# The same instructions in another order: an attention and expert-mixing kernel whose step order becomes a written list

## The chip, the cores and the metric

One core of one Trainium2 chip runs the whole program. The metric is device time in microseconds (us). Before the change three runs took 616.56 to 617.46 us, with a median of 617.3 us. The trace is of one profiled execution.

## The reference

Two stages follow each other. In the first, 64 heads (8 batches of 8, 576 positions of 64 numbers) go through a linear attention: q and k are projected to 128 features, the greatest absolute value of each row is taken off, and both signs of the exponential are kept.

```python
def phi(x):
    proj = np.einsum('bhsd,df->bhsf', x, w_phi)
    proj = proj - np.max(np.abs(proj), axis=-1, keepdims=True)
    return np.concatenate([np.exp(proj), np.exp(-proj)], axis=-1)
kv = np.einsum('bhsf,bhsd->bhfd', k_p, v)      # and z, the sum of k_p over s
num = np.einsum('bhsf,bhfd->bhsd', q_p, kv)    # divided by q_p . z
```

Its result x (8 batches of 576 x 512) goes through four softmax attentions, the experts, with a causal mask; for each position the two experts with the greatest gate logits are kept, weighted by a softmax over the two, and added after the projection `wo`.

```python
q, k, v = x @ wq[e], x @ wk[e], x @ wv[e]
a = softmax(where(causal, -1e9, 0.125 * q @ k.T))
out += gate_weight[e] * (a @ v @ wo[e])
```

## The kernel before, in words

The program is written as some twenty kinds of generators ("streams"). Each yields a `Step` that names the engine of the next piece of work, and then issues that piece. A `Plan` chooses which stream goes on next; the choice fixes the order in which every engine executes its instructions, since `in_order` (called at the end) ties each instruction to the one before it on its engine. No loop remains at run time.

The first stage works in 32 pairs of heads (p). `load_k`, `load_q` and `load_v` issue the transfers, on SyncE's queue but for the first two loads of q. `stream_k` projects k (line 509, a tiling of TensorE with 64 rows), `center` takes the greatest absolute value and subtracts it (VectorE, lines 564 and 578), ScalarE makes both exponentials (326); `key_sum` adds blocks of them on VectorE (546), and `stream_kv` multiplies them with v in four tiles of 32 columns (605, 622). The product is transposed on TensorE for the first six pairs (633), later on VectorE and through DRAM (641, `kvd`). `stream_q` projects q (509); `evac_u` copies the result from PSUM to `u`, on ScalarE (324) or VectorE (336); GpSimd finds the greatest value over all partitions (`partition_all_reduce`, 681); VectorE subtracts it (685); ScalarE makes the exponentials (326). `stream_n` makes the denominators (710) and numerators (721), also in 32-column tiles; `fractions` and `divide` form the quotient and split it into two parts, `xh` and `xl`.

The second stage works in 8 batches of 4 pairs, each batch in two groups of two experts, which makes 16 groups (n = 0 to 15). Products with `qk`, `vg` and `wo` use the full 128 x 128 tiling, three products of high and low parts each (315). The scores use 64-row tiles (838). Then follow the copy from PSUM (324 or 336), the mask on GpSimd (942), maxima on VectorE (955), an all-reduce on GpSimd into the one buffer `max` (959), the subtraction (963), exponentials (326), the addition of blocks into that same buffer `max` (975), their sums on TensorE (1001), the product with v (1030), `evac_y` (1044, 324, 319), the projection with `wo` (315), `evac_o` and the stores, which go through two buffers `ot`. A new all-reduce can overwrite `max` only after the sums of the group before have read it.

What sets the order before: `Plan.loop` estimates for each stream when its step could start, from assumed costs, keeps those within `WINDOW` of the earliest, and takes the one of the lowest position number. These numbers come from tables (`POS`, `POS1`, `BOFF`, `MOVE`) by pair and batch. Where a step may go to either engine (`copies`), the estimate also picks ScalarE or VectorE, with 544 ns against VectorE (`FLEX`). `keep_warm` fills TensorE with small products until the first x exists.

Of the kernel before, what the change touches and what calls it, by code (L numbers as in the profile page):

```python
# [12 lines left out]
ALU = mybir.AluOpType  # L13
# [5 lines left out]
NP = H // 2  # L19
# [21 lines left out]
HOT = 22.62  # L41
SLOPE = (-27.1, -45.11, 31.37, 22.04, 0.2)
# [5 lines left out]
FLEX = (544, -30)  # L48
QB = 1
PSUB = 0  # L50
# [4 lines left out]
WINDOW = 53.0  # L55
SWITCH = 43.0
SLACK = 150.0
LATE = (1200.0, 500.0)
PHASE = 0.0
ZEROS = 34.47  # L60

MOVE = {
# [10 lines left out]
    'evu': (21.12, -4.06, 14.36, -18.44, 5.1, 15.91, 29.23, -7.85, 16.87, -12.86, 9.23, -24.49, -1.82, -0.22, -20.76, 24.81, 11.28, -7.35, 2.92, 2.45, 9.93, -6.72, -3.41, -34.68, -21.04, 1.48, -2.83, 22.44, -22.76, -6.25, 15.97, -11.69,),  # L73
    'ph0': (-8.14, 0.95, 0.11, -1.26, 2.32, -7.14, 14.26, 1.03, -4.68, 5.71, 17.28, -2.71, 7.54, -8.69, 8.12, 18.24, -7.03, 16.87, -6.18, -9.54, -25.96, 24.71, -7.89, 12.56, -1.56, 10.54, -2, -6.36, -29.4, -8.19, -24.29, 4.42,),
    'ph1': (0.98, -31.26, 7.61, 13.17, -13.03, -6.78, -4.19, 30.31, 1.24, 14.84, -16.58, -8.83, -2.18, 2.26, -24.69, 4.64, 4.19, -14.28, -5.42, 5.41, 8.16, -8.76, -6.61, 2.72, -6.37, 21.76, -7.17, -16.16, -0.85, 16.73, 11.84, -11.68,),
    'cen': (-18.81, 6.49, -10.84, 12.73, -20.02, 8.22, 2.67, -4.13, -37.26, -31.66, -22.98, -21.09, -1.99, 11.55, -10.57, 24.02, 3.96, -3.59, 2.44, 14.24, 5.39, 33.73, 12.84, 2.35, -5.61, -5.03, -22.36, 21.58, -8.41, -5.42, -15.78, 16.67,),
    'evd': (-0.53, -8.66, 7.47, -22, -18.99, -9.4, -18.15, 12.47, -19.84, 8.28, -2.9, -3.62, 17.77, 27.72, -5.5, -22.57, 11.69, -3.3, -11.95, -21.43, -1.49, 34.49, 13.92, 18.59, 3.14, 4.37, 4.81, 2.48, 26.02, 6.28, 12.39, -10.59,),
    'n1': (7.63, -9.91, 2.94, 8.61, 6.97, 3.71, 0.17, -10.61, -19.77, -1.78, -4.43, -30.48, -18.43, 0.14, 9.45, -11.23, -16.35, -18.78, 7.28, 10.47, 7.42, -28.12, 5.4, 14, -24.35, -5.88, -12.01, -7.61, 17.16, -5.33, -22.39, -11.91,),
    'div': (-24.16, 1.89, 13.29, 2.53, 0.65, -0.28, 8.21, -7.67, -3.37, 4.47, -12.51, 7.23, 1.58, -6.78, 5.93, 2.54, 10.1, -14.14, -5.17, -6.51, 26.08, -8.09, -24.63, 7.57, 4.12, 2.66, -35.81, -1.48, 11.92, -19.86, -16.37, -36.85,),
# [6 lines left out]
    'gate': (19.49, -11.43, -6.09, 0.85, 5.59, 17.09, 4.34, 6.95,),  # L86
    't1': (6.21, -13.36, 7.09, -2.21, -6.96, -5.15, -13.11, -22.93,),
    'out': (0.94, -2.47, -1.22, -1.17, -4.2, 1.36, 15.49, 6.05,),
    'fin': (0, 0, 0, 0, 0, 0, 0, -0.18,),
}  # L90
POS1 = {'wq': 24.27, 'wv': 48.25, 'wo': 6.32, 'n0': -29.41, 'n1': 1.65, 'k': -1.55, 'q': -17.83, 'v': 6.22, 'kv': -23.07, 'z': 0.35, 'cen': -7.3, 'evu': -37.47, 'ph0': 25.81, 'ph1': 20.93, 'div': 3.92, 'evd': -3.25, 'lk': -12.81, 'lq': 47.36}
BOFF = (-5.07, 0.34, -2.66, -3.42, -4.38, 5.28, 25.26, 8.75)

POS = {'fin': 20.11, 'p0': -6.7, 'p1': -66.09, 'v0': 14.93, 'gate': -16.07, 's0': 3.48, 's1': -24.31, 'm0': 14.77, 'm1': 13.89, 't0': -38.13, 't1': 12.5, 'out': 23.34}
NPAIRS = B * NP
HEAD = 2.29
# [3 lines left out]
TRATE = 2.37  # L100
CHANGE = (150.0, 190.0)
PORT = 350.0
OTHER = 20.47
LDW = 109.0
PSUM_TILES = (("c", 8, 512),)


def moved(x, i):

    return MOVE[x][i] if x in MOVE else 0  # L110


def of_pair(x, p):

    return (p - HEAD if p < NP else p) + POS1[x] + moved(x, p)


def of_batch(x, b):
    return NP * b + BOFF[b] + POS[x] + moved(x, b)


class Step:

    def __init__(self, eng, needs=(), tag=None, pred=None, hot=False, port=False, tiling=(128, 128), n=1, slack=0.0, filler=False):
        self.eng, self.needs, self.tag, self.pred = eng, needs, tag, pred
        self.port, self.tiling, self.n = port, tiling if eng == 'PE' and (tag or tiling != (128, 128)) else None, n
        self.lead = HOT if hot else 0.0
        self.filler = filler  # L130
        self.slack = slack + (SLACK if eng == 'PE' else 0.0)


class Plan:


    HOP = {'PE': 200.0, 'DVE': 150.0, 'ACT': 150.0, 'POOL': 80.0, 'SP': 100.0}

    def __init__(self):
        self.warm, self.busy = False, []  # L140
        self.tiling = None
        self.rings = 0.0
        self.free = {e: 1470.0 if e == 'PE' else 600.0 for e in ('PE', 'DVE', 'ACT', 'POOL', 'SP')}
        self.ready = {}
        self.last = {}
        self.psum = {}
        self.streams = []
        self.pool = []
        self.done = set()
# [17 lines left out]
    def blocked(self, t):  # L167

        return PORT if any(a < t < b for a, b in self.pool) else 0.0

    def run(self, eng, cost, w=(), r=(), rows=128, tiling=(128, 128), port=False):
        if eng == 'PE' and tiling != self.tiling:
            cost += CHANGE[tiling == (128, 128)]
            self.tiling = tiling
# [7 lines left out]
        if port:  # L182
            cost += self.blocked(t)
        end = t + cost
        self.free[eng] = end
        if eng == 'POOL':
            self.pool = [*self.pool[-7:], (t, end)]
# [21 lines left out]
    def after(self, table, k, eng):  # L209
        t, by = table.get(k, (0.0, eng))  # L210
        if by == eng == 'PE':
            return t
        return t + self.HOP[by] + (100.0 if eng == 'PE' else 0.0)

    def spawn(self, gen, pos):
        s = [gen, None, pos]
        if self.advance(s, None):
            self.streams.append(s)

    def advance(self, s, value):  # L220
        try:
            s[1] = s[0].send(value)
            if isinstance(s[1], tuple):
                s[1], pos = s[1]
                s[2] = s[2] if pos is None else pos
# [931 lines left out]
```

## Time and profile before

| | |
|---|---|
| median of three runs | 617.3 us |
| profiled execution, span | 615.0 us |
| around the span, if that execution took the median | 2.3 us |
| TensorE busy | 600.5 us, 98% |
| VectorE busy | 557.3 us, 91% |
| ScalarE busy | 432.0 us, 70% |
| GpSimd busy | 245.0 us, 40% |
| chain that ended last | TensorE 74%, VectorE 15%, ScalarE 5% |

PE is TensorE, DVE VectorE, ACT ScalarE, POOL GpSimd, SP SyncE. Matmuls overlap in their pipeline, so the sum of their durations is more than the time that they take: what one costs in a row of equal ones is the distance between starts. The page does not give the profiled execution's whole time, only its span; the difference to the median is carried along unchanged.

### The profile page before, as it was taken

Reading aid. Unit: us, or ns where it says so; the run is one execution under the profiler, and the core shown is the slowest. Engines: PE = TensorE matmul, PEld = TensorE weight load, DVE = VectorE, ACT = ScalarE, POOL = GpSimd, SP = SyncE. Lnnn points to the kernel's source line nnn. Section 1 sums busy time; section 2 is a strip of 40 time slices with the busy share of each in tenths; the row PEclk is TensorE's granted clock in tenths of the full one; section 3 lists DMA queues with packets and bytes.
Section 4 is the critical chain, followed back from the end, with each engine's and each line's share of the span. In section 5 each row is a group of like instructions: output and inputs, shape, how many; then the busy total and the mean of one; then the engine's idle time right before and its main releaser. Section 6 shows DMA issues by size and latency. Waiting matters only on the chain.

```text
span 615.0 us, 19992 instructions
## 1 busy us (share of the span) xinstructions
PE 600.5 (98%) x8263; PEld 470.6 (77%) x8263; DVE 557.3 (91%) x1124; ACT 432.0 (70%) x1034; POOL 245.0 (40%) x167
## 2 busy tenths in 40 slices
PE   8999999999999999999999999999999999999987
PEld 7665788667796778768886868876889677878976
DVE  5899989999999999999899999999999998888793
ACT  4898786667687688677775885875796668556652
POOL 5635533453324644252333614418430706421420
PEclk9999999999999999999999999999999999999999
DMA  9553212253113431253214332144212311020022
GB/s 218 155 150 103 59 51 81 68 159 87 54 66 113 120 87 37 72 158 110 74 35 107 119 107 63 46 135 138 66 53 83 111 37 27 15 92 2 2 78 78
DMA packets 41610, 52.48 MB, mean 85 GB/s; under 512 B 21168, under 2 KB 24624, under 8 KB 41520
## 3 DMA queue, kind: packets, MB, share of 16 engines
q1 hardware_dynamic: 41200, 50.62, 28.5%
q8 instruction: 65, 1.06, 0.7%
q10 hardware_dynamic: 320, 0.59, 0.4%
q14 instruction: 25, 0.20, 0.1%
HBM read 36.64 MB, written 14.55 MB: 83 GB/s over the span
## 4 chain that ended last, share of the span: by engine, by line
PE 74%; DVE 15%; ACT 5%; DMA 2%; issue 2%; POOLq 1%; POOL 1%; SPq 0%; ACTq 0%; DVEq 0%
PE ps_c L315 29%; PE ps_c L509 9%; PE ps_c L605 9%; PE ps_c L721 7%; PE ps_c L1030 6%; PE ps_c L838 6%; PE ps_c L710 4%; DVE u L685 3%; DVE zs L546 2%; PE ps_c L622 2%; ACT ek L326 2%; PE ps_c L1001 1%; DVE s L963 1%; DVE ek L578 1%; DVE max L975 1%
## 5 line engine op out<-in xcount | busy, mean ns | idle before, releaser
L681 POOL PARTITION_ALL_REDUCE mx<-u x64 | 144.2, 2305 | 182.7 <-ACT u L324 165.9
L315 PE MATMUL ps_c<-xh,qk 128*128 128x320 f32 (+1 forms) x512 | 106.1, 298 | 0.0
L959 POOL PARTITION_ALL_REDUCE max<-top x16 | 59.9, 3745 | 101.5 <-DVE top L955 35.8
L315 PEld LDWEIGHTS ps_c<-xh,qk 128*128 128x128 f32 x512 | 82.7, 188 | 2.3 <-issue 0.7
L326 ACT ACTIVATE ek<-ek 128x1152 f32<-128x1152 f32 x64 | 75.0, 1171 | 5.7 <-DVE ek L578 5.0
L315 PE MATMUL ps_c<-xl,qk 128*128 128x256 f32 (+1 forms) x256 | 75.5, 295 | 0.0
L605 PE MATMUL ps_c<-ek,v_in 128*32 128x256 f32 x1280 | 75.4, 381 | 0.0
L963 DVE TENSOR_TENSOR s<-s,max 128x1152 f32<-128x1152 f32 (+4 forms) x80 | 68.3, 879 | 1.0 <-POOL max L959 1.0
L942 POOL TENSOR_SCALAR_AFFINE_SELECT s<-s 128x256 f32<-128x256 f32 (+1 forms) x80 | 41.5, 558 | 62.2 <-ACT s L324 61.9
L685 DVE TENSOR_TENSOR u<-u,mx 128x576 f32<-128x576 f32 x64 | 61.6, 975 | 3.9 <-POOL mx L681 3.9
L324 ACT COPY s<-ps_c 128x512 f32<-128x512 f32 (+4 forms) x152 | 52.7, 445 | 14.7 <-PE ps_c L838 14.4
L326 ACT ACTIVATE s<-s 128x1152 f32<-128x1152 f32 (+4 forms) x80 | 56.4, 740 | 8.6 <-DVE s L963 8.4
L605 PEld LDWEIGHTS ps_c<-ek,v_in 128*32 128x32 f32 x1280 | 39.7, 110 | 27.2 <-issue 1.3
L315 PE MATMUL ps_c<-vg,xh 128*128 128x260 f32 (+1 forms) x320 | 58.9, 286 | 0.3 <-ACT s L324 0.3
L564 DVE TENSOR_REDUCE pmax<-ps_c 128x4 f32<-128x512 f32 (+1 forms) x96 | 49.5, 539 | 8.1 <-PE ps_c L509 8.0
L315 PE MATMUL ps_c<-yh,wo 128*128 128x320 f32 (+1 forms) x256 | 53.1, 303 | 0.0
L326 ACT ACTIVATE mx<-u 128x576 f32<-128x576 f32 x64 | 43.9, 687 | 10.5 <-DVE u L685 10.4
L324 ACT COPY u<-ps_c 128x256 f32<-128x256 f32 (+1 forms) x127 | 41.6, 412 | 11.7 <-PE ps_c L509 11.4
L578 DVE TENSOR_TENSOR ek<-ps_c,pmax 128x512 f32<-128x512 f32 (+1 forms) x96 | 49.8, 537 | 0.0
L315 PEld LDWEIGHTS ps_c<-vg,xh 128*128 128x128 f32 (+1 forms) x320 | 47.4, 177 | 1.9 <-ACT s L324 0.8
L509 PEld LDWEIGHTS ps_c<-wf,k_in 64*128 64x128 f32 x576 | 41.9, 190 | 8.5 <-ACT u L324 3.0
L509 PE MATMUL ps_c<-wf,k_in 64*128 64x128 f32 x576 | 46.7, 283 | 1.5 <-ACT u L324 1.1
(124 smaller groups left out, 1399.4 us busy)
## 6 DMA issues: line engine op xcount, KB each, us to landing
v_in<-in_v_dram SPq DMA_DIRECT2D x32, 320.0 KB, 3.0
out_dram<-ot SPq DMA_DIRECT2D x32, 288.0 KB, 2.1
q_in<-in_qt_dram SPq DMA_DIRECT2D x60, 144.0 KB, 2.9
kvd<-kvt SPq DMA_DIRECT2D x104, 48.0 KB, 1.7
kv<-kvd SPq DMA_DIRECT2D x26, 192.0 KB, 2.6
k_in<-in_kt_dram SPq DMA_DIRECT2D x32, 144.0 KB, 2.8
k_in<-in_kt_dram SPq DMA_DIRECT2D x32, 128.0 KB, 2.8
q_in<-in_qt_dram ACTq DMA_DIRECT2D x4, 144.0 KB, 4.1
```

The costliest lines, as they stand in the source:

```text
L315: nc.tensor.matmul(o, a, b, start=start, stop=stop, skip_group_check=True)
L324: nc.scalar.copy(o, i)
L326: nc.scalar.activation(o, i, func, **kw)
L509: nc.tensor.matmul(o, a, b, start=True, stop=True, skip_group_check=True)
L564: dve(n * 128, [mk], [pk]).tensor_reduce(out=m[:, us], in_=src, axis=AX.X, op=ALU.max, apply_absolute_value=True)
L578: dve(n * 128, [e1k], [pk, mk]).tensor_tensor(out=ek2[p % EKB][:, 1, us, :], in0=src, in1=m[:, us].unsqueeze(2).to_broadcast([128, n, 128] ...
L605: nc.tensor.matmul(o[g, 0:2], v_in[:, 4 * h + t if t < 4 else 8 + h, k:64:2], ek[:, :, u_, :].rearrange("p c (w f) -> p c w f", w=4), star ...
L681: nc.gpsimd.partition_all_reduce(M, U, 128, bass_isa.ReduceOp.absmax)
L685: (nc.gpsimd if st.eng == 'POOL' else nc.vector).tensor_tensor(out=U, in0=U, in1=M, op=ALU.subtract)
L721: nc.tensor.matmul(ps[g:g + 32, 0:n], kvi[:, 2 * k + h, 32 * c:32 * c + 32], P_[h][c][:, s0:s1], start=c == 0, stop=c == 1, skip_group_che ...
L959: nc.gpsimd.partition_all_reduce(big.rearrange("p e s -> p (e s)"), top.rearrange("p e s -> p (e s)"), 128, bass_isa.ReduceOp.max)
L963: dve(2 * (S - 128 * j), [('d', x, j)], [('max', z)], 1.11, True).tensor_tensor(out=block(s_, j, None, rows(j)), in0=block(s_, j, None, ro ...
```

## The change

The tables and the choice go. Two strings stand in their place. Each character of `ORDER` is an index into the list of live streams, and the stream at that index goes on; each character of `SIDES` says for one step that could go either way whether it goes to ScalarE (0) or VectorE (1). The pieces of work, the tiles, buffers and transfers are those of before; the assumed costs in `plan.run` were changed as well, and still choose which free PSUM bank a step gets. The only instructions that differ in number are the fillers of `keep_warm` (117 before, 105 after), and 64 copies out of PSUM or between buffers that stand on VectorE instead of ScalarE (31 on VectorE before, 95 after).

```diff
+ORDER = (
+    r'11000000320000063655BEEE???66BA2B?@3BA555500EGG?00000000000000@A0B047D073DD0@@@?:@25766A@16:00:7I:ADC?4B6A5B15'
...
+SIDES = (
+    r'10000010101100000100011001000100000001011000000000001001001000000000000110000000000010000000000000000000000000'
...
     def loop(self):
-        while self.streams:
-            cand = []
...
-                t, eng = self.start(st)
-                cand.append((t + (SWITCH if st.filler or self.other(st) else 0.0), eng, s))
...
-            t0 = min(c[0] for c in cand) + WINDOW
-            _, eng, s = min((c for c in cand if c[0] <= t0), key=lambda c: (round(1e4 * (c[2][2] - c[2][1].lead + (OTHER if self.other(c[2][1]) else 0.0))), c[0]))
-            s[1].eng = eng
+        sides = iter(SIDES)
+        for c in ORDER:
+            s = self.streams[ord(c) - 48]
+            st = s[1]
+            assert st.pred is None or st.pred()
+            if isinstance(st.eng, tuple):
+                st.eng = st.eng[int(next(sides))]
             slot = None
...
     def copies(n):
-        return ('ACT', 52 + 0.83 * n), ('DVE', 65 + 1.04 * n + FLEX[0])
+        return 'ACT', 'DVE'
```

Line numbers of the changed kernel are some 36 to 46 lower than those of before: 509 is 471, 838 is 792, 315 is 279, 685 is 645, 963 is 917, 975 is 929, 1001 is 955, 1030 is 984.

First place, TensorE in the first third: the last block of a projection of k (one product with `wf` that stands alone). Before, it comes between the key sums and a numerator:

```order
L509 MATMUL ps_c3_66<-wf_118,k_in0_102 128x128
L622 MATMUL ps_c2_65<-zs_111,ones_112 32x4x32 x4
L622 MATMUL ps_c2_65<-ek0_108,sel_114 32x4x32 x4
L509 MATMUL ps_c4_67<-wf_118,k_in0_102 128x128
L721 MATMUL ps_c6_69<-mx30_139,kv1_120 32x256 x2
```

Now, at a like place of a later pair, such a block stands between two runs of scores:

```order
L792 MATMUL ps_c2_65<-qh0_159,kkl0_162 128x320
L792 MATMUL ps_c0_63<-ql0_160,kkh0_161 128x320
L792 MATMUL ps_c2_65<-ql0_160,kkh0_161 128x320
L471 MATMUL ps_c6_69<-wf_118,k_in1_103 128x128
L792 MATMUL ps_c7_70<-qh0_159,kkh0_161 128x448
```

What moved: the single block left a stretch of 32-column tiles, where it made TensorE change its tiling twice, for a stretch of 64-row tiles like its own. Counted over the whole order (64-row tiles of both lines taken as one kind, 32-column tiles as a second, full tiling as a third), the tiling changes 169 times before and 144 times after; behind the last scores 7 and 5 times.

Second place, VectorE behind the last scores (group 15, in s1; s0 holds group 14). Before:

```order
L955 TENSOR_TENSOR top0_155<-s1_154 128x2x448
L955 TENSOR_TENSOR top0_155<-top0_155,s1_154 128x2x320
L955 TENSOR_TENSOR top0_155<-top0_155,s1_154 128x2x192
L955 TENSOR_TENSOR top0_155<-top0_155,s1_154 64x2x64
L963 TENSOR_TENSOR s0_153<-s0_153,max0_156 64x2x64
L975 TENSOR_TENSOR max0_156<-s0_153 128x2x448
L975 TENSOR_TENSOR max0_156<-max0_156,s0_153 128x2x320
```

Now (909 is 955, 929 is 975):

```order
L909 TENSOR_TENSOR top0_155<-s1_154 128x2x448
L909 TENSOR_TENSOR top0_155<-top0_155,s1_154 128x2x320
L929 TENSOR_TENSOR max0_156<-s0_153 128x2x448
L929 TENSOR_TENSOR max0_156<-max0_156,s0_153 128x2x320
L909 TENSOR_TENSOR top0_155<-top0_155,s1_154 128x2x192
L909 TENSOR_TENSOR top0_155<-top0_155,s1_154 64x2x64
```

The two additions for group 14 moved ahead of the last two maxima of group 15, and the small subtraction of group 14 to an earlier place. On TensorE the sums that read these additions stand right behind the product with `vg` after the change; before, two units with `wo` stood between.

Third place, VectorE behind the last all-reduce, from the third subtraction of group 15 on. Before:

```order
L963 TENSOR_TENSOR s1_154<-s1_154,max0_156 128x2x320
L742 TENSOR_TENSOR ps_c7_70<-ps_c7_70,gc_166 128x18
L963 TENSOR_TENSOR s1_154<-s1_154,max0_156 128x2x192
L745 STREAM_TRANSPOSE rb0_157<-ps_c7_70 128x576
L963 TENSOR_TENSOR s1_154<-s1_154,max0_156 64x2x64
L975 TENSOR_TENSOR max0_156<-s1_154 128x2x448
L1044 TENSOR_TENSOR ps_c2_65<-ps_c2_65,rb0_157 128x256
L1044 TENSOR_TENSOR ps_c4_67<-ps_c4_67,rb0_157 128x320
L975 TENSOR_TENSOR max0_156<-max0_156,s1_154 128x2x320
```

Now:

```order
L917 TENSOR_TENSOR s1_154<-s1_154,max0_156 128x2x320
L917 TENSOR_TENSOR s1_154<-s1_154,max0_156 128x2x192
L917 TENSOR_TENSOR s1_154<-s1_154,max0_156 64x2x64
L702 TENSOR_TENSOR ps_c6_69<-ps_c6_69,gc_166 128x18
L929 TENSOR_TENSOR max0_156<-s1_154 128x2x448
L929 TENSOR_TENSOR max0_156<-max0_156,s1_154 128x2x320
L705 STREAM_TRANSPOSE rb0_157<-ps_c6_69 128x576
L998 TENSOR_TENSOR ps_c0_63<-ps_c0_63,rb0_157 128x256
```

The transpose into `rb0` and the two multiplications of group 14 moved behind both additions of group 15. On TensorE, the product of group 15 with v now follows its sums directly; before, two half units with `wo` (six products) stood between them.

## Rows read from the trace of the kernel before

**Rows 1.** The page, its first line and its busy times:
```profile
span 615.0 us, 19992 instructions
PE 600.5 (98%) x8263; PEld 470.6 (77%) x8263; DVE 557.3 (91%) x1124; ACT 432.0 (70%) x1034; POOL 245.0 (40%) x167
```

**Rows 2.** Windows: length, busy time (and instructions) by engine, granted clock, DMA share, GB/s:
```profile
30.00:585.00 555.00, 549.23 (x7549) 428.96 (x7542) 517.02 (x1029) 400.10 (x963) 223.45 (x152) 1.00 0.28 80
...
598.00:602.50 4.50, 3.20 (x34) 2.54 (x38) 2.64 (x7) 1.54 (x6) 0.00 (x0) 0.62 0.17 66
```

**Rows 3.** Chain that ended last, pieces on TensorE: start, us, what:
```profile
10.10 4.29 PE ps_c L315 x75
...
183.94 1.80 PE ps_c L315 x12
185.74 2.84 PE ps_c L1030 x56
188.58 1.94 PE ps_c L721 x32
...
387.37 7.33 PE ps_c L315 x60
394.70 2.08 PE ps_c L721 x32
396.78 2.16 PE ps_c L605 x40
```

**Rows 4.** Timeline around 221 to 226 us, GpSimd, VectorE, TensorE (start, us, instruction, idle):
```profile
221.25 4.47 POOL L681 PARTITION_ALL_REDUCE mx<-u  x2 [8.45 <-ACT u L324]
...
221.52 1.85 DVE L685 TENSOR_TENSOR u<-u,mx 128x576 f32<-128x576 f32 x1
223.47 0.44 DVE L732 STREAM_TRANSPOSE wided<-ps_c 128x288 f32<-128x288 f32 x1
223.91 1.58 DVE L685 TENSOR_TENSOR u<-u,mx 128x576 f32<-128x576 f32 x1
225.42 0.77 DVE L745 STREAM_TRANSPOSE rb<-ps_c 128x576 f32<-128x576 f32 x1
...
226.24 0.47 PE L838 MATMUL ps_c<-qh,kkh 64*128 64x448 f32 x1 [1.26 <-DVE rb L745]
```

**Rows 5.** Instructions of tile u on VectorE: duration ns min/median/max:
```profile
L685 DVE TENSOR_TENSOR u<-u,mx x64: 709/747/2255, 11.5 to 519.5; 128x576 f32<-128x576 f32 x64
L336 DVE COPY u<-ps_c x1: 474/474/474, 413.7 to 413.7; 128x320 f32<-128x320 f32 x1
```

**Rows 6.** Groups by line and shape: busy us, mean ns, idle before:
```profile
L685 DVE TENSOR_TENSOR u<-u,mx 128x576 f32<-128x576 f32 x64 | 61.6, 975 | 3.9 <-POOL mx L681 3.9
L732 DVE STREAM_TRANSPOSE wided<-ps_c 128x288 f32<-128x288 f32 x32 | 15.0, 467 | 1.1 <-PE ps_c L710 1.0
```

**Rows 7.** Chain that ended last, from the last scores on:
```profile
575.94 2.66 PE ps_c L838 x35
...
581.44 1.16 DVE top L955
...
585.94 0.84 DVE max L975
...
588.31 3.65 POOLq L1152
...
595.63 0.69 DVE rb L745
...
597.94 0.49 DVE ps_c L1044
598.43 0.74 DVE max L975
...
599.30 1.40 PE ps_c L1001 x24
600.70 1.74 PE ps_c L315 x6
602.44 2.84 PE ps_c L1030 x56
```

More of the change, by code (lines that the diff above doesn't have):

```diff
@@ L99, with change_cost @@
 RATE = 2.18
[L100 to L103, printed above, removed]
+TRATE = 2.4
+EXIT = 95.0
+ENTRY = {'F': 102.0, 'R': 99.0, 'S': -31.0, 'C': 23.0, 'Q': 10.0}
 LDW = 109.0
+ROWS = (0.997, 1.008)
 PSUM_TILES = (("c", 8, 512),)
[L108 to L119, printed above, removed]
-class Step:
[L126 to L131, printed above, removed]
+def change_cost(a, b):
+    if a is not None and a[:2] == b[:2]:
+        return 0.0
+    kind = ('C' if b[0] == 128 else 'Q') if b[1] < 128 else 'F' if b[0] == 128 else 'S' if len(b) > 2 else 'R'
+    return EXIT + ENTRY[kind]
@@ L181, in run @@
             cost = self.clocked(t, cost, rows)
-        if port:
+        if eng == 'DVE' and port:
             cost += self.blocked(t)
+            self.shared = (t, t + cost)
+        if eng == 'POOL' and self.shared[0] < t < self.shared[1]:
+            t = self.shared[1]
         end = t + cost
@@ L231, in release @@
         self.psum[tag].append(t)
-    def start(self, st):
-        best = None
-        for eng, cost in st.eng if isinstance(st.eng, tuple) else ((st.eng, 0.0),):
-            t = self.free.get(eng, 0.0)
-            for k in st.needs:
-                t = max(t, self.after(self.ready, k, eng) + st.slack)
-            if st.tag is not None:
-                t = max(t, sorted(self.after(self.last, k, eng) for k, _ in self.psum[st.tag])[st.n - 1])
-            if eng == 'DVE' and st.port:
-                cost += self.blocked(t)
-            if best is None or t + cost < best[0]:
-                best = t + cost, t, eng
-        return best[1:]
@@ L506, in half_mm @@
     def half_mm(o, a, b, n, w, r, alone=1.0):
-        plan.run('PE', 2 * alone * n / TRATE + 3, [w], r, tiling=(64, 128))
+        plan.run('PE', alone * ROWS[n == 128] * (2 * n / 2.37 + 3), [w], r, tiling=(64, 128))
         nc.tensor.matmul(o, a, b, start=True, stop=True, skip_group_check=True)
@@ L531, in stream_k @@
             cols = [slice(0, 9)] if not CACT else [slice(4 * t, min(9, 4 * t + 4)) for t in range(3) if t not in CACT]
-            yield Step('ACT', [e1k], pred=lambda: all(('center', p, t) in done for t in range(3)))
+            yield Step('ACT', pred=lambda: all((('center', p, t) in done for t in range(3))))
             for us in cols:
@@ L608, in stream_kv @@
             if adds:
-                yield Step('PE', ['zs'], pred=has('zs', p), hot=True, slack=LATE[1], tiling=(128, 32))
+                yield Step('PE', pred=has('zs', p))
             first = 1 if KADD == 3 else 2
@@ L895, in gates @@
         G = 'gate'
-        yield Step('DVE', ['lg'], pred=lambda: all(('v', b, j) in done for j in range(NJ)) and (not b or ('gate', b - 1) in done))
+        yield Step('DVE', pred=lambda: all((('v', b, j) in done for j in range(NJ))) and (not b or ('gate', b - 1) in done))
         dve(80, [G], ['lg'], port=True).tensor_tensor(out=ge, in0=lg.unsqueeze(3).to_broadcast(sh4),
@@ L917, in gates @@
         done.add(('gw', b))
-        kc, ps = yield Step('PE', [G], 'c', tiling=(128, 32), slack=LATE[0])
+        kc, ps = yield Step('PE', 'c')
         o = ps[:, 0:40].rearrange("p (g j a d) -> p g j a d", g=2, a=2, d=2)
@@ L924, in gates @@
             nc.tensor.matmul(o[r:r + 32, :, :, a, half], ident[:, c:c + 32], w2[:, e], start=True, stop=True, skip_group_check=True)
-        st = Step(copies(40), [kc], pred=lambda: not b or (('gated', 2 * b - 1) in done and ('gated', 2 * b - 2) in done), hot=True)
+        st = Step(copies(40), pred=lambda: not b or (('gated', 2 * b - 1) in done and ('gated', 2 * b - 2) in done))
         yield st
@@ L938, in mask @@
         sk = [('S', x, IN_BANK[j][0], e) for e in range(2)]
-        yield Step('POOL', sk, pred=lambda: all(('S', n, IN_BANK[j][0], e) in done for e in range(2)))
-        plan.run('POOL', 260 + 1.3 * 2 * w, [('m', x, j)], sk)
+        yield Step('POOL', pred=lambda: all((('S', n, IN_BANK[j][0], e) in done for e in range(2))))
+        plan.run('POOL', 230 + 0.65 * 2 * w, [('m', x, j)], sk, port=100 + 1.3 * w)
         d = ss[x][:w, :, KEYS[j]:KEYS[j] + w]
@@ L989, in sums @@
         s_, need = ss[x], [('P', x, 0)] + ([('max', n % MB)] if SADD else []) + [('P', x, j) for j in range(SADD + 1, NJ)]
-        pk, ps = yield Step('PE', need, 'c', lambda: ('acc', n) in done and all(('P', n, j) in done for j in range(NJ)), tiling=(128, 32)), of_batch(f't{g}', b)
+        pk, ps = yield Step('PE', 'c', lambda: ('acc', n) in done and all((('P', n, j) in done for j in range(NJ))))
         pieces = [(block(s_, j), 64 * j, j == 0, j == NJ - 1) for j in range(NJ)]
```

313 lines of the change are left out of this document (152 added, 161 removed), and 16 rows, old and new, of the table MOVE.

## Prediction
> **What bounds the kernel now.** I read the page's busy times first, then the windows, then the chain of waits, and last the timelines at places where TensorE waits. TensorE is busy for 600.5 of 615.0 us, VectorE for 557.3, ScalarE for 432.0 [rows 1]. The middle part, from 30 to 585 us, is 555.0 us long, and TensorE idles there for 555.0 - 549.2 = 5.8 us, VectorE for 555.0 - 517.0 = 38.0 us [rows 2]. So over nine tenths of the run the end is set by how fast TensorE gets through its list. What an order can win there is of two kinds: the cost of changing the tiling, which hides inside "busy", and the few waits. The reader should see in the chain that a block of equal products costs more when it follows another tiling: 32 numerator products take 2.08 us behind the full-tiling product with `wo` or `qk`, and 1.94 behind other 32-column products; 56 products with v take 2.84 behind the full tiling [rows 3].
>
> Behind the last scores, which end at 575.94 + 2.66 = 578.60 us, the picture changes: 36.4 us of the span are left, and most of that is a chain through VectorE, GpSimd and TensorE for the last group of experts [rows 7]. [...]
>
> A third thing can be seen at 221 to 226 us. A subtraction on VectorE (line 685) that usually takes 747 ns [rows 5] takes 1.85 and 1.58 us while GpSimd's all-reduces run, the transpose into `rb` queues behind it, and TensorE idles 1.26 us for that transpose [rows 4]. VectorE's busy time thus holds time in which it is only held up. For line 685 alone that is 64 x (975 - 747 ns) = 14.6 us [rows 5, 6].
>
> **The change part by part.** All sums start from the profiled execution: 615.0 us of span, and 2.3 us around it if it took the median of 617.3.
>
> *Tiling changes.* I counted them in the two orders: 169 and 144, of which 7 and 5 stand behind the last scores; 23 fewer in the part that TensorE bounds. The price of one: 2.08 - 1.94 = 0.14 us [rows 3]. The single projection block between scores in the new order shows how they were saved. Entering the full tiling may cost a little more and leaving it less; both ends of the price, 0.05 and 0.25 us, are my estimate around that one difference. 23 x 0.14 = 3.2 us less (1.2 to 5.8).
>
> *Fillers.* 12 fewer; 75 took 4.29 us [rows 3], so 12 x 0.057 = 0.7 us. They only fill time in which TensorE waits for the first pairs, so the gain may be nothing. I take 0.7.
>
> *Waits in the middle.* 5.8 us are visible [rows 2]. A wait costs more than its idle time, since the pipeline fills again: the product behind the wait at 226.24 us took 0.47 us [rows 4], where products in a full row start 7.33 / 60 = 0.12 us apart [rows 3]. About 0.35 us for each of some eleven waits gives 3.8 us, together 9.6 us at most. At the other end the new order has as many waits as the old one, and the gain is nothing (it can be below nothing: that is the third rival). No row shows the new waits. I take the middle, 4.8 us, because the visible wait that I followed came from a held-up subtraction, and an order can set such a subtraction beside the all-reduce or behind it.
>
> *Copies that move to VectorE.* 64 copies; the one of this kind in the trace took 474 ns for 320 columns [rows 5], and many are shorter, so 0.43 us each, 27.5 us (64 x 0.474 = 30.3 at most). They leave ScalarE, which had 30% of its time free. On VectorE they fall into 38.0 us of idle time and into the 14.6 us and more in which two-input operations are held up. I cost them at nothing for the end; the cover is that idle time, and if it is gone they cost up to 27.5 us. Queued behind each of them on VectorE are the subtractions, additions and row maxima that give back PSUM banks, and TensorE waits for those.
>
> [...] In rows 4 the transpose into `wided`, which reads PSUM, ran in 0.44 us under an all-reduce, no slower than its mean of 467 ns [rows 6], while the subtraction of two SBUF tiles was held up. [...]
>
> *The tail.* First, the last all-reduce starts 588.31 - 578.60 = 9.7 us after the last scores [rows 7]. Its maxima begin at 581.44, and with the two additions the row of VectorE ends at 585.94 + 0.84 = 586.78, of which some 0.2 us is the small subtraction that now stands earlier; but it still had to wait until TensorE had done two units with `wo` and the sums of group 14. Now 60 products with `vg` follow the scores, 60 x 0.12 = 7.3 us, and then the sums at once, about 1.1 us: all-reduce at 8.5 us behind the scores, 1.2 us earlier. Second, from the chain between all-reduce and the last additions, the transpose into `rb` (0.69 us) and a multiplication (0.49 us) are gone: 1.2 us. Third, six products between the sums and the product with v (1.74 us at the lower clock) are gone: 1.7 us. They come later, where stores already set the pace; I give back 0.5 us. Together 1.2 + 1.2 + 1.7 - 0.5 = 3.6 us less (1.5 to 5.5). Late next are the last two multiplications of group 14, now behind the additions; they have the 2.84 us of the product with v [rows 7] to be done in.
>
> *Sum.* 615.0 - 3.2 - 0.7 - 4.8 - 3.6 = 602.7 us of span; with 2.3 us around it 605.0 us.
>
> **The rivals.** *Only what can be counted.* The waits of the middle stay: 617.3 - 3.2 - 0.7 - 3.6 = 609.8 us. For it: two in-order engines at 98% and 91% leave little room, and one stall moved is often another made. Against it: TensorE's waits have few and plain causes.
>
> *Nearly all waits go.* 617.3 - 3.2 - 0.7 - 9.6 - 3.6 = 600.2 us, and with the upper ends of the tail and the tiling price 598. For it: all waits together are under 2% of the span. Against it: the first 60 us, in which VectorE and ScalarE feed the first pairs, leave no choice.
>
> *VectorE becomes the bound (slower).* The place is the middle part. If VectorE is held up as often as before, 27.5 of its 38.0 us of idle time go, 10.5 us or 2% are left, and an in-order engine with so little slack is late for the row maxima, the subtractions and the quotients. If half of the added work then shows up as waits of TensorE, the time is 617.3 - 7.5 + 13.7 = 623.5 us. It decides as soon as more than 7.5 us of new TensorE waits appear. For it: VectorE is the next busiest engine, and the change loads it. Against it: the held-up time can shrink by about as much as is added.
>
> *The order does nothing.* Waits that the list did not foresee eat the counted gains: 616 to 618 us. Against it: fewer tiling changes are certain, and the tail is a chain of single rows.
>
> **How the numbers follow.** The forecast of 605.0 us gets 0.47, only the countable parts 0.19, nearly all waits 0.14, VectorE as the bound 0.13, nothing 0.07. About 0.2% of the time, 1.2 us, can be told from no change. Faster: 0.47 + 0.19 + 0.14 + 0.01 = 0.81; the same 0.05; slower 0.13 + 0.01 = 0.14. The range for 8 in 10 goes from 598 us, the bottom of the third case, to 616 us, which leaves out VectorE as the bound and most of the last case. The forecast's own range is 602 to 608.
>
> **What would show it.** Right: the last scores end near 570 us instead of 578.6; between them and the end of the span about 33 us; TensorE's idle time in the middle falls to about 3 us; the mean of the subtraction (now line 645) falls from 975 towards 800 ns; no stretch at the lower clock, or a shorter one, before the last product with v. VectorE's busy time then stays below 575 us. Wrong: VectorE's busy time at 585 us or more, with TensorE waits on VectorE that sum to over 10 us, would be the third rival; a last all-reduce that starts 9.7 us or more behind the last scores would refute the tail; equal TensorE waits with a gain near 7 us would be the first rival.

## The result and the profile after

The changed kernel takes 624.62 us (median of four runs, 623.74 to 625.54) against 616.93 us before (614.86 to 617.46): ratio 1.0131, 95% interval 1.0109 to 1.0154. It is 1.3% slower, where 2% faster was forecast. The profiled execution took 624.03 us, 2.4 us of it outside the span (2.3 had been carried along for before). The two spans differ by 6.6 us, the medians by 7.7.

The page of the changed kernel, its first line, busy times, and the chain that ended last by engine and by line:

```profile
span 621.6 us, 20010 instructions
...
PE 600.5 (97%) x8251; PEld 468.9 (75%) x8251; DVE 590.5 (95%) x1188; ACT 404.8 (65%) x970; POOL 248.6 (40%) x167
...
PE 51%; DVE 32%; issue 8%; POOL 5%; ACT 2%; DMA 1%; SPq 1%; DVEq 0%; ACTq 0%; POOLq 0%
PE ps_c L279 17%; PE ps_c L471 7%; PE ps_c L681 6%; PE ps_c L567 6%; DVE zs L508 6%; PE ps_c L792 4%; PE ps_c L984 4%; DVE u L645 4%; PE ps_c L670 3%; DVE s L917 3%; DVE top L909 3%; POOL mx L643 3%; DVE pmax L526 2%; DVE ek L540 2%; PE ps_c L584 1%
```

TensorE is busy as long as before [rows 1]; VectorE 33.2 us longer. VectorE's part of the chain has doubled from 15% to 32%, and its largest line there is 508, the key-sum additions. The windows of the changed kernel (columns as in [rows 2]):

```profile
30.00:585.00 555.00, 541.03 (x7449) 419.56 (x7451) 538.41 (x1072) 367.17 (x885) 224.86 (x148) 1.00 0.29 82
...
600.00:606.00 6.00, 4.25 (x78) 3.24 (x80) 5.66 (x14) 3.96 (x11) 0.00 (x0) 1.00 0.14 53
```

In the middle TensorE idles 555.0 - 541.0 = 14.0 us instead of 5.8 [rows 2], VectorE 16.6 instead of 38.0. The next rows are VectorE's instructions of the tiles u and zs in the changed kernel (duration min/median/max in ns), and the same groups by line with busy us, mean ns:

```profile
L645 DVE TENSOR_TENSOR u<-u,mx x64: 705/744/1893, 12.2 to 545.6; 128x576 f32<-128x576 f32 x64
...
L508 DVE TENSOR_TENSOR zs<-zs,ek x56: 640/677/2554, 51.3 to 524.9; 128x512 f32<-128x512 f32 x56
L508 DVE TENSOR_TENSOR zs<-ek x28: 636/680/2401, 50.1 to 521.3; 128x512 f32<-128x512 f32 x28
...
L645 DVE TENSOR_TENSOR u<-u,mx 128x576 f32<-128x576 f32 x64 | 56.9, 901 | 0.6 <-POOL mx L643 0.6
L508 DVE TENSOR_TENSOR zs<-zs,ek 128x512 f32<-128x512 f32 x56 | 50.4, 899 | 0.3
L508 DVE TENSOR_TENSOR zs<-ek 128x512 f32<-128x512 f32 x28 | 26.3, 938 | 0.0
```

The key sums in the kernel before, which the prediction leaves out:

```profile
L546 DVE TENSOR_TENSOR zs<-zs,ek x56: 644/680/1904, 50.7 to 509.8; 128x512 f32<-128x512 f32 x56
L546 DVE TENSOR_TENSOR zs<-ek x28: 639/679/1702, 50.0 to 507.0; 128x512 f32<-128x512 f32 x28
...
L546 DVE TENSOR_TENSOR zs<-zs,ek 128x512 f32<-128x512 f32 x56 | 42.4, 757 | 0.5
L546 DVE TENSOR_TENSOR zs<-ek 128x512 f32<-128x512 f32 x28 | 21.6, 772 | 0.6 <-ACT ek L326 0.4 <-PE ps_c L622 0.2
```

An undisturbed addition takes 680 ns in both (the median). Over that, the means give 56 x 77 + 28 x 92 ns = 6.9 us before and 56 x 219 + 28 x 258 ns = 19.5 us now: time in which an addition was only held up (the expectations below put it at 7.2 and 20.3 us). The subtraction of u went the hoped-for way, from 14.6 us [rows 5, 6] to 64 x (901 - 744 ns) = 10.0 us. Of the additions that take over 0.85 us, 9 run under an all-reduce before and 20 now; of the subtractions over 0.92 us, 13 and 8. So the new order took subtractions out from under the all-reduces and put additions there. What is held there are operations with two operands in the SBUF: in the changed kernel 37 of them start in the first 40% of an all-reduce, and 35 take over 0.2 us longer than their median; of the 116 operations that start there and read PSUM, none takes more than 0.02 us longer.

What one such addition does, in the changed kernel's timeline at 389 us (start, us, engine, line, instruction, idle before):

```profile
389.10 3.58 POOL L913 PARTITION_ALL_REDUCE max<-top  x1 [5.33 <-DVE top L909]
...
389.35 2.40 DVE L508 TENSOR_TENSOR zs<-ek 128x512 f32<-128x512 f32 x1
...
391.68 0.41 DVE L300 COPY s<-ps_c 128x256 f32<-128x256 f32 x1
...
392.14 0.41 PE L792 MATMUL ps_c<-qh,kkh 64*128 64x320 f32 x1 [1.01 <-DVE s L300]
```

The addition takes 2.40 us under an all-reduce; the copy of the scores queues behind it; TensorE waits 1.01 us for the bank that the copy gives back. The copy is one of the kind that the change moved to VectorE. TensorE's waits in the changed kernel (what waited, for what: us in total, times, longest us), the first three, and the two longest for VectorE in the kernel before:

```profile
PE ps_c L792 <- DVE kkl L283: 2.1, 2, 1.5
PE ps_c L681 <- DVE xl L283: 2.0, 2, 1.2
PE ps_c L584 <- DVE zs L508: 1.9, 3, 1.1
```

```profile
PE ps_c L838 <- DVE rb L745: 1.7, 2, 1.3
...
PE ps_c L838 <- DVE xl L319: 1.0, 1, 1.0
```

From 30 to 585 us all waits of TensorE for VectorE sum to 13.4 us, before to 2.9 us. The first three groups are for VectorE, and only the third for an addition; what the others wait for stood in VectorE's queue. Six waits of this stretch last 1.0 us or more, 7.2 us together: five end 0.1 to 4.4 us behind a held addition, the sixth 0.9 us behind a held subtraction. For the place of the loss, the products of the scores in the last part of each kernel, after and before (duration min/median/max in ns, first and last start in us):

```profile
L792 PE MATMUL ps_c<-qh,kkh x24: 188/318/466, 572.3 to 587.2; 64*128 64x320 f32 x8, 64*128 64x192 f32 x4, 64*128 64x256 f32 x4, 64*128 64x448 f32 x4
```

```profile
L838 PE MATMUL ps_c<-qh,kkh x24: 189/318/469, 563.4 to 578.3; 64*128 64x320 f32 x8, 64*128 64x192 f32 x4, 64*128 64x256 f32 x4, 64*128 64x448 f32 x4
```

The last one starts 8.9 us later; 34.4 us of the span follow it instead of 36.7. So 8.9 us are lost ahead of it and 2.3 won behind.

### The profile page after: what moved, and what is told of

It reads as the page before. It is cut to its first block, busy times and chain, and to the rows that moved or that the text cites. A ratio compares the mean times of both kernels' runs of the same rounds, so it can differ in the third digit from the quotient of the medians.

```text
span 621.6 us, 20010 instructions
## 1 busy us (share of the span) xinstructions
PE 600.5 (97%) x8251; PEld 468.9 (75%) x8251; DVE 590.5 (95%) x1188; ACT 404.8 (65%) x970; POOL 248.6 (40%) x167
## 4 chain that ended last, share of the span: by engine, by line
PE 51%; DVE 32%; issue 8%; POOL 5%; ACT 2%; DMA 1%; SPq 1%; DVEq 0%; ACTq 0%; POOLq 0%
PE ps_c L279 17%; PE ps_c L471 7%; PE ps_c L681 6%; PE ps_c L567 6%; DVE zs L508 6%; PE ps_c L792 4%; PE ps_c L984 4%; DVE u L645 4%; PE ps_c L670 3%; DVE s L917 3%; DVE top L909 3%; POOL mx L643 3%; DVE pmax L526 2%; DVE ek L540 2%; PE ps_c L584 1%
## 5 line engine op out<-in xcount | busy, mean ns | idle before, releaser
L643 POOL PARTITION_ALL_REDUCE mx<-u x64 | 145.5, 2313 | 131.9 <-ACT u L288 89.6
L913 POOL PARTITION_ALL_REDUCE max<-top x16 | 57.7, 3609 | 98.6 <-DVE top L909 62.8
L896 POOL TENSOR_SCALAR_AFFINE_SELECT s<-s 128x256 f32<-128x256 f32 (+1 forms) x80 | 45.4, 595 | 120.1 <-ACT s L288 82.8
L290 ACT ACTIVATE ek<-ek 128x1152 f32<-128x1152 f32 x64 | 74.9, 1170 | 17.6 <-DVE ek L540 16.8
L917 DVE TENSOR_TENSOR s<-s,max 128x1152 f32<-128x1152 f32 (+4 forms) x80 | 70.1, 901 | 0.9 <-POOL max L913 0.9
L290 ACT ACTIVATE s<-s 128x384 f32<-128x384 f32 (+4 forms) x80 | 57.5, 743 | 15.2 <-DVE s L917 14.3
L288 ACT COPY s<-ps_c 128x448 f32<-128x448 f32 (+4 forms) x137 | 51.0, 434 | 24.9 <-PE ps_c L792 24.7
L645 DVE TENSOR_TENSOR u<-u,mx 128x576 f32<-128x576 f32 x64 | 56.9, 901 | 0.6 <-POOL mx L643 0.6
L279 PE MATMUL ps_c<-yh,wo 128*128 128x320 f32 (+1 forms) x256 | 52.6, 299 | 0.0
L540 DVE TENSOR_TENSOR ek<-ps_c,pmax 128x512 f32<-128x512 f32 (+1 forms) x96 | 51.2, 542 | 0.7
L508 DVE TENSOR_TENSOR zs<-zs,ek 128x512 f32<-128x512 f32 x56 | 50.4, 899 | 0.3
L984 PE MATMUL ps_c<-s,vs 128*32 128x320 f32 (+4 forms) x896 | 47.2, 357 | 3.2 <-ACT ot L288 1.7
```

The lines of the kernel that those rows point to most:

```text
L279: nc.tensor.matmul(o, a, b, start=start, stop=stop, skip_group_check=True)
L290: nc.scalar.activation(o, i, func, **kw)
L508: dve(512, ['zs'], ekk, 1.11, True).tensor_tensor(out=zs, in0=zs if a > 1 else x[:, :, :, 0], in1=x[:, :, :, a], op=ALU.add)
L540: dve(n * 128, [e1k], [pk, mk]).tensor_tensor(out=ek2[p % EKB][:, 1, us, :], in0=src, in1=m[:, us].unsqueeze(2).to_broadcast([128, n, 128] ...
L643: nc.gpsimd.partition_all_reduce(M, U, 128, bass_isa.ReduceOp.absmax)
L645: dve(S, [uk], [mk], port=True).tensor_tensor(out=U, in0=U, in1=M, op=ALU.subtract)
```

## The experiments

Two causes were on the table: theory A, the 64 copies that now load VectorE (the prediction's third rival), and theory B, the order itself. Within B the question became what in the order costs: operations held under the all-reduces, or the length of the all-reduce for those that wait for it. `ORDER` and `SIDES` of any mixture can be written as such strings, so whole orders, pieces of them and sides could be exchanged. Medians in us; the kernel before, measured beside them, took 616.37 to 616.75:

| run | order | change | time | ratio to before, 95% |
|---|---|---|---|---|
| e3 | old | as a list | 617.14 | 1.0003 to 1.0022 |
| e2 | old | new sides | 634.29 | 1.0276 to 1.0307 |
| e1 | new | old sides | 627.62 | 1.0167 to 1.0198 |
| e4 | new | copies to ScalarE | 628.30 | 1.0172 to 1.0210 |
| f1 | old, new tail | | 614.58 | 0.9960 to 0.9984 |
| i1 | new head, old middle, new tail | | 618.54 | 1.0016 to 1.0042 |
| g1 / g2 | new / old | short all-reduces | 605.73 / 612.25 | 0.979 to 0.986 / 0.990 to 0.995 |
| n1 | new | short, two spare ones | 618.35 | 1.0021 to 1.0046 |
| o1 / o2 | new / old | short, one spare | 611.70 / 614.40 | 0.991 to 0.994 / 0.994 to 0.998 |
| j1 / j2 / j3 | new / old / f1 | key sums as reductions | 659.15 / 654.07 / 652.79 | 1.068 to 1.071 / 1.059 to 1.063 / 1.057 to 1.063 |
| k1 / k2 | new / old | one-operand key sums | 612.85 / 616.81 | 0.993 to 0.996 / 1.000 to 1.001 |
| l1 | new | eleven sums later | 618.34 | 1.0023 to 1.0050 |
| l2 | f1 | twelve held ones later | 616.56 | 0.9989 to 1.0010 |

**Sides and order apart (e1 to e4).** The edit is in the strings alone:

```diff
 ORDER = ( ... )            # e1, e4: new; e2, e3: the recorded order of before
 SIDES = ( ... )            # steps on VectorE: e1, e3 29 as before; e2 93 as after; e4 7
```

> The new step order, with every copy that may go either way on the engine it had before (29 steps on VectorE instead of 93). Theory A (VectorE's added load made the kernel slow): about 611 us, since the fewer tiling changes, fillers and the shorter tail remain (about 5 us) and VectorE is as free as before. Theory B (the order itself makes VectorE late, by additions and maxima that are held up under GpSimd's all-reduces, and the sides matter little): 620 to 625 us.

> The old step order as a list, with the copies on the engines that the changed kernel gives them (93 steps on VectorE). Theory A: slower than before, 624 to 630 us, VectorE's busy time near 580 us. Theory B: within 2 us of before, 615 to 619 us.

> The old step order and the old sides, written as a list in the changed kernel; only the choice among free PSUM banks follows the changed kernel's assumed costs. Both theories: the time of before, 615 to 619 us. A time of 621 us or more would make the bank choice a cause of its own.

> The new step order with every copy out of PSUM on ScalarE (7 flexible steps left on VectorE, all between SBUF tiles). Theory A: as fast as with the old sides or faster, 606 to 612 us. Theory B: 618 us or more. If ScalarE is what then comes late, its waits grow and the time lies above that of the new order with the old sides.

e3 gives the time of before to 0.1%: writing the order down costs next to nothing. Theory A fell for the new order. With the copies back on ScalarE it did not recover, it lost 3 us more (e1), and with 22 more steps there it is no faster (e4). The window of e1 and its larger group of additions show it:

```profile
30.00:585.00 555.00, 540.75 (x7401) 420.23 (x7401) 520.89 (x1013) 382.29 (x940) 223.23 (x148) 1.00 0.28 82
...
L508 DVE TENSOR_TENSOR zs<-zs,ek 128x512 f32<-128x512 f32 x56 | 53.2, 951 | 0.3
```

VectorE has 34.1 us of idle time again, TensorE still idles 14.3 us, and the additions take 53.2 + 23.6 = 76.8 us, as in the changed kernel (76.7). An engine with room to spare can be late. e2 fits neither theory: in the old order the same copies cost 17 us against e3. A part of these may be clock: the mean granted clock is 0.988 in each of e2's four runs, and 0.996 or 0.997 in e3's ten. TensorE's longest waits for VectorE in e2 are 3.2, 1.9 and 1.7 us, in e3 2.6, 1.3 and 1.0; that these waits lowered the clock is not shown, and how much it cost was not separated. Sides and order belong together.

**Pieces of the order (f1, i1).** f1 takes the old order up to the last scores and the new one behind them; i1 also takes the new one up to the first finished scores.

> The old order up to the issue of the last scores, and from there the new order (sides as each had them). The new tail took 34.1 us from the last scores to the end of the span, the old one 36.4 us. If the tail is a gain of its own, 614 to 615 us, 2 us below before. If it only looked shorter because VectorE had more work done or the last scores came late, 616 to 618 us.

> The new order up to the first scores (they ended 2.3 us earlier in the changed kernel than in the old order as a list), then the old order for all that is left, and from the last scores on the new order. If gains of single stretches add up, 612 to 614 us. If a stretch's gain is given back where the orders meet (what one order has done early the other has to wait for elsewhere), 616 us or more.

The new tail is worth 2.2 us, and f1 beats both kernels. The head does not add to it: 2.3 us ahead of e3 at the end of the first scores, i1 is 3.9 us behind it at the second group's, and stays there. In front of the old middle the new head was no gain.

**Short all-reduces (g1, g2).** The 64 all-reduces of the q side run over 64 of 576 columns; the maxima of the other columns are left out, and the subtraction uses these 64 for all columns.

```diff
-nc.gpsimd.partition_all_reduce(M, U, 128, bass_isa.ReduceOp.absmax)
+nc.gpsimd.partition_all_reduce(M[:, 0:64], U[:, 0:64], 128, bass_isa.ReduceOp.absmax)
```

> The changed kernel, but the 64 all-reduces of q's features run over 64 of 576 columns, and the subtraction uses those 64 maxima for all columns; the rest of the maxima is left out. [...] Theory B1 (the new order is slow since more of VectorE's two-input operations fall under these all-reduces, 20 us of hold-ups in key-sum additions instead of 7): the changed kernel gains more from this than the old order does, and ends below it, by some 4 us. Theory B2 (the new order leaves too little slack between engines, hold-ups or not): it stays slower than the old order with the same cut, by 4 us or more.

> The old order as a list with the same cut of the all-reduces to 64 of 576 columns, the rest of the maxima left out: the comparison for the new order with that cut. 595 to 612 us, since 20 us of hold-ups on VectorE under these all-reduces go and part of TensorE's waits with them. Theory B1: 4 us or so above the new order with the cut; theory B2: 4 us or more below it.

The sign turns. The old order gains 4.9 us (against e3), the new one 18.9, and now it is the faster by 6.5 us. Two rows of the chain by engine, and of the windows, of g1:

```profile
PE 83%; DVE 8%; issue 4%; POOL 2%; ACT 2%; DMA 1%; ACTq 0%; POOLq 0%; DVEq 0%
...
30.00:585.00 555.00, 550.83 (x7651) 435.96 (x7651) 526.77 (x1103) 376.88 (x912) 145.58 (x154) 1.00 0.28 81
```

VectorE's part of the chain falls from 32% to 8%, and TensorE idles 4.2 us. Left open was whether it was the all-reduce's hold on VectorE that had gone, or its latency. Against latency stand VectorE's own waits: the subtractions of the changed kernel waited for their all-reduces twice, 0.6 us in all (the last column of their group above), those of g1 once, 0.4 us.

**GpSimd's time given back (n1, o1, o2).** Behind each short all-reduce follow spare ones on a scratch tile that nothing waits for: two of 256 columns in n1, one of 384 in o1 and o2 (the other columns' maxima left out as in g1).

> The new order with all-reduces over 64 of the 576 columns (605.7 as measured), and behind each two spare all-reduces of 256 columns on scratch tiles, for which nothing waits; the maxima of the other columns are left out, as in the run with short all-reduces. GpSimd is busy about as long as in the changed kernel, but the all-reduce that is waited for is short. Theory of the hold-ups: VectorE is held again, in other places than by the long ones, 617 to 625. Theory of the latency: within 3 us of 605.7.

> The new order with each all-reduce over 64 of 576 columns (605.7 as measured; the maxima of the other columns are left out) and behind it one spare all-reduce of 384 columns on a scratch tile that nothing waits for, so that GpSimd is busy about as long as with full all-reduces while the awaited one stays at about 0.8 us. Theory of the hold-ups: 617 to 623. Theory of the latency: 605 to 608.

> The same in the order of before (612.3 with short all-reduces alone). Theory of the hold-ups: 614 to 618, and o1 no longer below it as g1 was below g2. Theory of the latency: 612 to 613, and o1 some 6 us below it.

n1 lost 12.6 us of g1's gain; its subtractions waited for an all-reduce once, 2.8 us. o1 lost 6.0 us and o2 2.2. That is less than the theory of the hold-ups expected (o1 617 to 623), and o1 stays below o2. The spare all-reduce (in o1 1808 ns in the mean, with no idle time of GpSimd before it) starts behind the short one (730 ns), so it can hold other instructions than the full one (2313 ns) did. The key sums in g1, and then in o1:

```profile
L508 DVE TENSOR_TENSOR zs<-zs,ek 128x512 f32<-128x512 f32 x56 | 41.9, 748 | 0.3
L508 DVE TENSOR_TENSOR zs<-ek 128x512 f32<-128x512 f32 x28 | 21.0, 752 | 0.3 <-ACT ek L290 0.2
```

```profile
L510 DVE TENSOR_TENSOR zs<-zs,ek 128x512 f32<-128x512 f32 x56 | 44.5, 794 | 0.3
L510 DVE TENSOR_TENSOR zs<-ek 128x512 f32<-128x512 f32 x28 | 24.2, 863 | 0.0
```

The additions take 62.9 us in g1, 68.7 in o1, 70.8 in n1 and 76.7 in the changed kernel; in the old order 59.3 in g2, 62.2 in o2 and 64.3 in e3. Within each order the times rise with them, so o1 fell short because its spare all-reduces held less. The subtractions' busy time rises as well (48.1, 52.6, 54.2 and 56.9 us in the new order), so these runs speak for hold-ups but do not tell which of the two operations matters.

**Key sums without hold-ups (j1 to j3, k1, k2).** The first try takes two reductions instead of three additions:

```diff
-dve(512, ...).tensor_tensor(out=zs, in0=zs if a > 1 else x[:, :, :, 0], in1=x[:, :, :, a], op=ALU.add)
+if a < 3:
+    dve(1024, ...).tensor_reduce(out=zs[:, a - 1], in_=x[:, a - 1].rearrange("p h a f -> p h f a"), axis=AX.X, op=ALU.add)
```

> The changed kernel, in which the sum of a pair's exponentials over its tiles is taken by two reductions, each with one operand from the SBUF, instead of three additions with two operands; same result, all-reduces at full length. Theory of the hold-ups (VectorE's two-input operations, the key-sum additions above all, are held under GpSimd's all-reduces, and the new order puts more of them there): the 20.3 us of hold-ups that the key sums have in the changed kernel go, the time falls by 6 to 14 us, to 611 to 618, and it comes level with or below j2's. Theory of the latency (the long all-reduce itself comes late for the chain that waits for it, whatever VectorE does meanwhile): within 3 us of 624.6, and still some 7 us above j2.

> The same edit in the order of before (written as a list, 617.1 as measured). Theory of the hold-ups: the key sums have 7.2 us of hold-ups in this order, so there is less to win: 3 to 5 us, 612 to 614. Theory of the latency: within 2 us of 617.

> The same edit in the old order with the new tail (614.6 as measured). Theory of the hold-ups: about 610 to 612, as the tail's 2.2 us and the key sums' 3 to 5 us lie in different stretches. Theory of the latency: 614 to 615.

All three missed, for a reason that neither theory had: such a reduction takes 1995 ns, where the kernel's own estimate for it, 65 + 1.04 ns for each of 1024 elements, is 1130. The group in j1:

```profile
L509 DVE TENSOR_REDUCE zs<-ek 128x256 f32<-128x1024 f32 x56 | 111.2, 1995 | 0.0
```

That is 111.2 us instead of 50.4 + 26.3 = 76.7, and the 34.5 us more are the 34.5 us by which j1 is slower than the changed kernel. In j2 the old order pays less: 45.9 us more of key sums (110.2 instead of 64.3 in e3) and 36.9 us more time. The runs tell nothing of the dispute. So k1 and k2 replace each addition, in its place, by a reduction of one operand of 640 elements (128 contiguous ones, read five times); the sums over the key tiles are left out.

```diff
-dve(512, ...).tensor_tensor(out=zs, in0=zs if a > 1 else x[:, :, :, 0], in1=x[:, :, :, a], op=ALU.add)
+dve(512, ...).tensor_reduce(out=zs[:, 0, 0, 0:5], in_=x[:, 0, 0, a].unsqueeze(1).to_broadcast([128, 5, 128]), axis=AX.X, op=ALU.add)
```

> The changed kernel with each of the 84 key-sum additions replaced, in the same place, by a reduction of 640 elements with one operand from the SBUF (about as long as an undisturbed addition, 0.68 us; the sums over the key tiles are left out, the denominators are a constant). The all-reduces keep their full length. Theory of the hold-ups: the 20.3 us that the additions were held go, most of it returns to the end: 608 to 616, and the gap to k2 shrinks from 7.5 us to 3 or less, or turns. Theory of the latency (or of the order in itself): within 3 us of 624.6, and 6 us or more above k2.

> The same edit in the order of before, written as a list. Theory of the hold-ups: 7.2 us of them go here, 611 to 614. Theory of the latency: 615 to 617, as only the duration of the replaced instruction can differ.

The instructions of the tile zs and the window, in k1:

```profile
L509 DVE TENSOR_REDUCE zs<-ek x84: 756/807/823, 50.2 to 513.6; 128x5 f32<-128x640 f32 x84
...
30.00:585.00 555.00, 549.13 (x7578) 429.41 (x7577) 537.31 (x1089) 375.16 (x904) 224.94 (x154) 1.00 0.29 82
```

None of 84 is held: the longest takes 823 ns, where an addition took up to 2554. The all-reduces are as long as ever, yet 11.8 us come back, the new order is 4.0 us faster than the old one, and TensorE's idle time is 5.9 us as in the kernel before. VectorE is as busy as in the changed kernel (537.3 and 538.4 us), and its subtractions are held no less (930 ns in the mean, 901 in the changed kernel): what counts is not the load but the place and length of the additions' stalls. k2 missed its 611 to 614; the replacement takes 807 ns and not 680, so that 84 x 0.127 = 10.7 us of work took the place of 6.9 us of hold-ups.

**The places alone (l1, l2).** All instructions stay; in l1 eleven key-sum additions that were held stand two or three VectorE instructions later, in l2 (from f1) five additions and seven subtractions of u one to three later.

```diff
 ORDER = ( ... )            # l1: e.g. step 0 of key_sum(24), the addition at 389.35 us,
                            # behind the copy of the scores and yl instead of ahead of them
```

> The changed kernel with all its instructions; eleven key-sum additions that were held in its trace (11.6 us over the undisturbed 0.68 us each) stand two or three VectorE instructions later, behind such as read PSUM. Theory of the hold-ups: VectorE does those under the all-reduce and the additions after it, so 4 to 9 us come back: 615 to 620. If only the number of operations counts, or the moved additions meet the next all-reduce instead: 623 to 626.

> The old order with the new tail (614.6 as measured), with five key-sum additions and seven subtractions of the q side that were held (some 10 us over their usual durations) moved one to three VectorE instructions later in the same way. Theory of the hold-ups: 2 to 5 us less, 610 to 613. If the places alone do not decide: 614 to 616.

l1 gives back 6.3 us without a change of any instruction. Its additions, by group:

```profile
L508 DVE TENSOR_TENSOR zs<-zs,ek 128x512 f32<-128x512 f32 x56 | 44.0, 786 | 0.3
L508 DVE TENSOR_TENSOR zs<-ek 128x512 f32<-128x512 f32 x28 | 23.1, 825 | 0.0
```

The busy time of the additions fell by 76.7 - 67.1 = 9.6 us. l2 missed: two us slower than f1. Its moves took hardly any hold-up away: the subtractions lost 2.2 us (61.5 to 59.3), the additions nothing (64.3 and 64.8). Its scores are 1.0 us behind f1's at the third group and 1.7 at the sixth and at the last. Which of the twelve moves did that was not tried; that a later subtraction also delays the exponentials that read it may be the cause, but is not shown. So places alone are worth 6.3 of the 7.7 us that the new order lost to the old one, but a later place is not a gain in itself.

## Why the prediction was wrong

The step that failed is the term "Waits in the middle": 4.8 us less, bounded by 9.6 us less on one side and on the other by "the new order has as many waits as the old one, and the gain is nothing". It came out as 14.0 - 5.8 = 8.2 us more idle time. The 0.35 us beyond its idle time that the upper end gives to each wait was an estimate; at the wait before 226.24 us it is some 0.2 (the starts around it lie 1.62 us apart, those of the row before it 0.15, and 1.26 were idle). Of the 18.9 us by which the span missed, 17.6 lie ahead of the end of the last scores (569.9 us by the sum, 587.5 measured). The bracket stopped at nothing and left everything beyond to a rival; and it rested on the subtraction alone, though additions of two SBUF tiles stood in the same trace with the same long tail (up to 1904 ns over a median of 680). The new order made the subtraction better and the additions worse. Without the additions' hold-ups 11.8 us of the 19.6 by which the time missed come back (k1), and by other places for eleven of them alone 6.3 (l1). The 598 us at the bottom of the range was a slip in the sum: with the two upper ends that it names it is 595.7.

*Tiling changes and fillers*, 3.9 us less. They can't be seen in the changed kernel under the 8.9 us lost ahead of the last scores. With short all-reduces the new order leads by 6.5 us, 2.2 of which the tail is worth in f1; the 4.3 us left are near these 3.9. They lie where such a gain would: up to the end of the last scores TensorE idles 3.8 us in g1 and 4.4 in g2, but is busy for 564.2 and 568.0. That agrees, but no run changed the tiling alone.

*Copies*, costed at nothing. Right for the new order, and better than that: taking them back costs 3 us (e1). Wrong as a rule: in the old order they cost 17 us (e2). The cover named, 38.0 us of idle time, is not what decides.

*The third rival*, VectorE as the bound, had the time nearly to the microsecond (623.5) and its sign: VectorE busy over 585 us, TensorE waiting for it. Its cause was wrong, as it laid the lateness on the 27.5 us of copies, and e1 has that without them; so the number was luck. Its argument against itself, that "the held-up time can shrink by about as much as is added", was the step to test: for subtractions and additions together it grew, from 14.6 + 6.9 = 21.5 to 10.0 + 19.5 = 29.5 us.

*The tail*, 3.6 us less, gave 2.3, and 2.2 in f1. The last all-reduce starts 8.7 us behind the last product of the rows above instead of 10.1, so the first term (1.2) held. What follows lost some of its part. Behind the last all-reduce of the changed kernel:

```profile
595.89 3.58 POOL L913 PARTITION_ALL_REDUCE max<-top  x1 [3.64 <-PE ps_c L955]
...
596.56 1.53 DVE L851 TENSOR_TENSOR ge<-vs 128x80 f32<-128x80 f32 x1
598.13 0.24 DVE L853 TENSOR_TENSOR ge<-ge,tri 128x80 f32<-128x80 f32 x1
...
601.20 0.41 DVE L300 COPY ot<-ps_c 128x256 f32<-128x256 f32 x1
601.53 3.74 DVE L917 TENSOR_TENSOR s<-s,max 128x1152 f32<-128x1152 f32 x5
```

The all-reduce ends at 599.47, but the first subtraction starts at 601.53: the small operations of the expert weights, the first of them itself held (1.53 us against a median of 0.23), stand between. Before, eight of these thirteen were done when the all-reduce started at 588.37, one of the rest was held (1.56 us), and VectorE still waited for the all-reduce at the end:

```profile
591.27 0.27 DVE L739 RECIPROCAL ps_c<-ps_c 128x18 f32<-128x18 f32 x1
591.99 3.10 DVE L963 TENSOR_TENSOR s<-s,max 128x1152 f32<-128x1152 f32 x3 [0.45 <-POOL max L959]
```

The step "late next" had named two multiplications; it was these. The clock did what was forecast: 1.00 granted from 600 to 606 us, where it had been 0.62 in the like stretch [rows 2] and 0.50 from 599 to 602 us.

*What was held, and how long.* What was held in the changed kernel were additions and subtractions of two SBUF tiles (19.5 and 10.0 us over their medians), and not the operations that read PSUM, the copies out of it among them (none of 116 by more than 0.02 us). Of the changed kernel's additions that ran under an all-reduce and took over 0.85 us, 20 in all, each ended before it did: the 16 under an all-reduce of the q side by 0.30 us, whether they had started 0.1 or 1.6 us behind its start, and the four under one into `max` by 0.93 us:

```profile
352.35 2.14 POOL L643 PARTITION_ALL_REDUCE mx<-u  x1 [0.44 <-ACT u L288]
...
352.52 1.67 DVE L508 TENSOR_TENSOR zs<-ek 128x512 f32<-128x512 f32 x1
```

Here 354.49 - 354.19 = 0.30 us; with 0.68 us for the work itself, taken in one piece, the addition ran from 0.98 us before the end of the all-reduce on; by this estimate it was held for about half of it. So none of the 20 was held to the end of its all-reduce, as far as the profile's spans on GpSimd, which are rough, can be trusted. Reductions with one operand in the SBUF, in the same places, were not held in k1: the longest of 84 took 823 ns, the median 807.

## What to carry to other kernels

Before a reordering is costed, list every operation that another engine can hold (here: two SBUF operands under an all-reduce on GpSimd, 35 of 37 in the changed kernel), and ask of each where the new order puts it; a median far below the mean or the maximum marks them (677 ns against 899 and 2554). An order that an engine must keep is judged by the longest stall ahead of what others wait for, not by an engine's idle time. Two orders with their sides are not exchanged piece by piece: of four mixtures (e1, e2, f1, i1) only the new tail was worth having.

## What had not been expected of the hardware

A reduction of groups of four terms that lie 512 bytes apart takes 1995 ns for 1024 elements per partition, one of five groups of 128 contiguous elements 807 ns: 1.95 against 1.26 ns an element. Whether the distance or the short groups make the difference was not tried. And even a small operation with two SBUF operands can be held as long as a large one, as the comparison of 80 elements in the changed kernel is, once of eight times (1.53 us, where the addition of 512 at 352.52 us took 1.67). Less its usual 0.23 us it ran from 1.97 us behind the start of the last all-reduce on, and the addition at 389.35 us, less its 0.68, from 1.97 us behind the start of its own:

```profile
L851 DVE TENSOR_TENSOR ge<-vs x8: 225/234/1534, 106.9 to 596.6; 128x80 f32<-128x80 f32 x8
```
